# Expert 0's second layer by seven block products, with the attention pieces placed in other slots

## Chip, cores and metric

The kernel runs on one core of a Trainium2 chip. The metric is the device time of one execution in microseconds (us). A figure of a version is the median of several runs; a profile is one further execution with the hardware profiler on. The engines are called TensorE (PE in the profile, PEld for its weight loads), VectorE (DVE), ScalarE (ACT), GpSimd (POOL) and SyncE (SP). GpSimd and SyncE here mostly issue transfers (DMAs).

## What is computed

Attention over pooled keys and values, and then four "experts" of two layers each, whose outputs are summed with normalised weights:

```python
k_p = k.reshape(B, H, Sp, pool, D).mean(axis=3)      # B, H, S, D = 8, 8, 576, 64; pool = 8
v_p = v.reshape(B, H, Sp, pool, D).mean(axis=3)
scores = scale * np.matmul(q, k_p.transpose(0, 1, 3, 2))
attn = softmax(scores)
x = np.matmul(attn, v_p)                             # as (4608, 512), one row a token
p = domain_probs / (domain_probs.sum(-1, keepdims=True) + 1e-09)
for e in range(4):                                   # w1: (4, 512, 1024), w2: (4, 1024, 512)
    h = np.maximum(x @ w1[e], 0.0)
    out += p[:, e:e + 1] * (h @ w2[e])
```

The two layers of the experts are nearly all of the arithmetic.

## The kernel before

**Chunks and steps.** The 4608 tokens are nine chunks of 512: chunks 0 to 7 take 512 tokens of one batch each, chunk 8 the 64 left over of each batch (`x_rem`). A step is a chunk and an expert, `(c, e)`, 36 in all in order (`steps`, L891). In a step TensorE computes the first layer of `(c, e)` and, between its products, the second layer of the step before. Each step has two halves, `j = 0, 1`.

**First layer by seven products.** `up_seven` (L713) computes a half of the hidden tile `H_sb` by seven block products in place of eight (a Strassen-like scheme): `product` (L638) issues 8 matmuls of 256 columns. The combinations of weight blocks are made once (`combine_w1`), those of the activations per chunk (`forms_of`, four VectorE operations, L608). A product that others need too is copied from PSUM by ScalarE (`keep`, L688, into a buffer `r`), and VectorE adds it and applies the relu (`relu_sum`, L692).

**Second layer, two ways.** `down` (L816) is the plain one: for each of four rows of 128 tokens 8 matmuls of 512 columns (L823), then `merge` (L830), which scales by the token's weight. For expert 0 `merge` starts the accumulator `acc` with a scaled copy on ScalarE (L834); for the others VectorE multiplies and adds (L837); after expert 3 SyncE writes the rows out (L845). `up_down` (L744) is the other: first layer of this step and second layer of the step before, both by seven products, in an order written out by hand. Its second-layer products are calls of `half` (4 matmuls of 256 columns, L761). It needs four sums of hidden blocks (`sums_of`, L700; operations L707 to L710 on VectorE, the second of them in place in `H_sb`), made at the end of the step in which the hidden tile was finished, and combined second-layer weights `w2_t` (`combine_w2`, L624). `splits` (L697) says for which steps this holds: experts 1 and 2 (`SPLIT`, L49) in chunks 1 to 8, so `up_down` runs in the steps of experts 2 and 3, and `up_seven` with `down` in those of experts 0 and 1.

**Points and slots.** Work that is not part of this runs at points. `point` (L896) issues what is placed under the running number `at`; `slot` (L902) first takes one piece from a queue `forms_due` and then does the same. Either way of doing a step passes 16 points, every second one a slot. `attention(c)` (L536) returns the pieces for batch `b = c + 1` under a number `n`, which is placed at point `2n + 1` of the chunk: `n` 0 to 7 falls into the step of expert 0, 8 to 15 into that of expert 1, and so on. The pieces are: sums over pooled keys and values on VectorE (`key_parts`, `value_parts`), transposes by DMA on SyncE (`keys` to `kpT`, `queries` to `qT`, `turn` to `xT`), `scores` (4 matmuls and an exponential on ScalarE, L276), `context` (8 matmuls, then a reciprocal and a product on VectorE, L376, L377), loads on GpSimd, and in odd chunks the left-over tokens (`rem_queries`, `rem_scores`, `rem_context`, `rem_turn`).

**What orders the work.** Each engine does its instructions in the order of the program; semaphores order the engines. `scores`, `context` and their remainder forms share one PSUM tile of two banks (`psum_a`); `g`, `d`, `s` of a half take three banks of `psum_h`; the second layer takes three of `psum_o`. The lines that set the placing:

Of the kernel before, what the change touches and what calls it, by code (L numbers as in the profile page):

```python
# [11 lines left out]
ALU = mybir.AluOpType  # L12
# [6 lines left out]
def kernel(  # L19
# [29 lines left out]
    SPLIT = (1, 2)  # L49
# [12 lines left out]
    accpool = ctx.enter_context(tc.tile_pool(name="accpool", bufs=5))  # L62
    rpool = ctx.enter_context(tc.tile_pool(name="rpool", bufs=4))
# [37 lines left out]

    def load_later(b, half):
        load_half(b, k, "kraw", half)
        load_half(b, v, "vraw", half)
# [376 lines left out]
    def warm(n):  # L481
        bank = psum_o.tile([P, NT], F32, tag="o_ps", name="o_ps")
        for _ in range(n):
            nc.tensor.matmul(bank[:], lhsT=zeros[:, 0:P], rhs=zeros[:])
# [51 lines left out]
    def attention(c):  # L536

        lo, hi = halves
        b = c + 1
        plan = {}  # L540

        def add(n, *what):
            plan.setdefault(n, []).extend(what)

        if c % 2:
            i = c // 2
            add(18, lambda: rem_queries(i))
            add(23, lambda: rem_scores(i))
            add(26, lambda: rem_context(i))
            add(27, lambda: rem_turn(i))  # L550
        if b == B:
            for part in forms_of(B):
                add(31, part)
            return plan
        if c == 1:
            add(0, lambda: queries(b), *key_parts(b)[:2])
            add(1, *key_parts(b)[2:])
            add(1, lambda: keys(b), lambda: loads_wait(b))
            add(1, lambda: (load_q(b + 1), load_q_rem(b + 1)))
        else:  # L560
            add(0, key_parts(b)[1], lambda: keys(b))
        scored, valued, mixed = 7, 9 if c > 1 else 6, 11
        for pair in range(NPAIR):
            add(scored + pair, lambda pair=pair: scores(b, pair))
        for n, part in enumerate(value_parts(b)):
            add(valued + n, part)
        if b + 1 < B:
            add(12, lambda: queries(b + 1))
            add(17, lambda: load_later(b + 1, 0))
            if b + 2 < B:  # L570
                add(19, lambda: (load_q(b + 2), load_q_rem(b + 2)))
            add(19, lambda: load_later(b + 1, 1))
            add(30, key_parts(b + 1)[0])
        for r in range(NR):
            add(mixed + r, lambda r=r: context(b, r))
            add(mixed + 1 + r, lambda r=r: turn(b, r))
        for n, part in enumerate(forms_of(b)):
            add((20, 21, 28, 29)[n], part)
        return plan
# [103 lines left out]
    def bank():  # L683
        return psum_h.tile([P, 2, TH], F32, tag="h_ps", name="g_ps")
# [11 lines left out]

    def splits(c, e):  # L697
        return c > 0 and e in SPLIT

# [13 lines left out]
    def up_seven(c, e, j, between):  # L713

        H_sb = hidden_of(c, e)
        top, low = H_sb[:, 2 * j:2 * j + 2], H_sb[:, 4 + 2 * j:6 + 2 * j]

        g, d, s = bank(), bank(), bank()
        product(c, e, j, 1, g, True)
        r1 = keep(g)  # L720
        between(0)
        product(c, e, j, 2, s, True)
        relu_sum(top[:, :, 0:TH], s, r1)
        product(c, e, j, 6, g, False)
        r2 = keep(g)
        between(1)
        product(c, e, j, 5, d, True)
        product(c, e, j, 7, g, False)
        r3 = keep(g)
        relu_sum(low[:, :, TH:NT], d, r3)  # L730
        between(2)
        product(c, e, j, 4, g, False)
        relu(low[:, :, 0:TH], g)
        between(3)
        product(c, e, j, 3, d, False)
        later = sums_of(c, e) if j and splits(c, e) else None
        if later:
            later[0]()
        relu_sum(top[:, :, TH:NT], d, r2)
        if later:  # L740
            for part in later[1:]:
                part()

    def up_down(c, e, j, dc, de):  # L744
# [5 lines left out]
        upper, lower = slice(TH + j * P, TH + (j + 1) * P), slice(j * P, (j + 1) * P)  # L750
        acc_u, acc_l = accs[(dc, 2 + j)], accs[(dc, j)]
# [29 lines left out]
        r2 = keep(g)  # L781
        slot()
# [5 lines left out]
        add(acc_l[:], prob_l, one[:])  # L788
# [21 lines left out]
        add(acc_u[:], prob_u, two[:])  # L810
# [3 lines left out]
    sums = {}  # L814

    def down(c, e, j, n):  # L816

        first = (0, 3, 7, 12, 16)
        for at in range(first[n], first[n + 1]):
# [7 lines left out]
            if fc == FCH - 1:  # L827
                merge(c, e, r, sums[r])
# [22 lines left out]
    zeros = const.tile([P, NT], BF16, name="zeros")  # L851
    pool_map = const.tile([FR, FT, SP], BF16, name="pool_map")
    ENG = mybir.EngineType
    with tc.manual_schedule(engines={ENG.PE, ENG.DVE, ENG.Activation, ENG.Pool, ENG.SP}):
        nc.vector.memset(zeros[:], 0.0)
        nc.vector.memset(pool_map[:], 1.0)
# [3 lines left out]
        for hs in halves:  # L860
            load_first(k, "k", hs)
        nc.gpsimd.affine_select(
            out=pool_map[:], in_=pool_map[:], compare_op=ALU.is_ge, fill=0.0,
# [3 lines left out]
            out=pool_map[:], in_=pool_map[:], compare_op=ALU.is_ge, fill=0.0,  # L867
# [39 lines left out]
        for s in range(len(steps) + 1):  # L907
# [24 lines left out]
            elif s == 5:  # L932
                forms_due.extend(w[3:] + nothing[:2] + combine_w2(SPLIT[0]))
                placed.setdefault(at + 5, []).extend(combine_w2(SPLIT[1], nc.gpsimd))
# [58 lines left out]
```

## Time and profile before

| | |
|---|---|
| median of 5 runs | 518.27 us (517.82 to 519.21) |
| the profiled execution | 518.79 us, of which the span from first to last instruction is 517.1 us |
| mean granted TensorE clock | 0.996 of full |
| matmuls: L644, 256 columns | 1056 + 696 + 96 recorded, mean 272 to 273 ns |
| matmuls: L823, 512 columns | 598 recorded, mean 379 ns |
| weight loads, 128 columns | 98 ns |
| `relu_sum` L692, x166 | 687 ns |
| `keep` L688, x166 | 585 ns |
| scaled copy of expert 0, L834, x36 | 690 ns |
| accumulate of 512, L767 x64 and L837 x44 | 746 ns |
| accumulate of 256, L767 x64 | 478 ns |
| sums of hidden blocks, L707 to L710, x16 each | 685 to 692 ns |
| exponential L276, x28 | 1019 ns |

A mean of a matmul is its latency; matmuls overlap, so the pitch of a stream is shorter and is read from the starts in the order of time. Some matmul records are missing from a trace, which leaves apparent gaps of one matmul's length. Busy shares are means over the whole span; where work ends up late is read from a step's own order of time.

The busy tenths in 40 slices show TensorE at 9 almost throughout, VectorE between 4 and 8 and ScalarE between 4 and 6 after the start:

```profile
PE   8899989999999999999999999999999999999996
PEld 3656544588757875788668866886688668866883
DVE  2434889878758864877577856776578546764674
ACT  3554434655475546554565546553665346534650
```

### The profile page before, as it was taken

Reading aid. Unit: us, or ns where it says so; the run is one execution under the profiler, and the core shown is the slowest. Engines: PE = TensorE matmul, PEld = TensorE weight load, DVE = VectorE, ACT = ScalarE, POOL = GpSimd, SP = SyncE. Lnnn points to the kernel's source line nnn. Section 1 sums busy time; section 2 is a strip of 40 time slices with the busy share of each in tenths; the row PEclk is TensorE's granted clock in tenths of the full one; section 3 lists DMA queues with packets and bytes.
Section 4 is the critical chain, followed back from the end, with each engine's and each line's share of the span. In section 5 each row is a group of like instructions: output and inputs, shape, how many; then the busy total and the mean of one; then the engine's idle time right before and its main releaser. Section 6 shows DMA issues by size and latency. Waiting matters only on the chain.

```text
span 517.1 us, 10085 instructions
## 1 busy us (share of the span) xinstructions
PE 501.5 (97%) x4125; PEld 363.7 (70%) x4171; DVE 341.4 (66%) x633; ACT 267.4 (52%) x467; POOL 71.0 (14%) x81
## 2 busy tenths in 40 slices
PE   8899989999999999999999999999999999999996
PEld 3656544588757875788668866886688668866883
DVE  2434889878758864877577856776578546764674
ACT  3554434655475546554565546553665346534650
POOL 8362101812003000020030001100000000000000
PEclk9899999999999999999999999999999999999999
DMA  9999998596339232961498047701210110011003
GB/s 132 206 206 205 201 161 156 89 117 63 77 80 134 26 46 78 141 62 23 108 109 89 2 117 89 74 11 56 58 24 1 41 53 1 11 42 41 1 1 81
DMA packets 82973, 41.57 MB, mean 80 GB/s; under 512 B 46560, under 2 KB 78304, under 8 KB 82928
## 3 DMA queue, kind: packets, MB, share of 16 engines
q0 software_dynamic: 41584, 22.65, 35.2%
q1 hardware_dynamic: 41344, 18.29, 18.0%
q8 instruction: 32, 0.52, 0.4%
q14 instruction: 13, 0.11, 0.1%
HBM read 45.16 MB, written 9.44 MB: 106 GB/s over the span
## 4 chain that ended last, share of the span: by engine, by line
PE 84%; DVE 10%; issue 2%; ACT 2%; DMA 1%; POOL 1%; POOLq 0%; ACTq 0%; DVEq 0%
PE g_ps L644 34%; PE o_ps L823 24%; PE u_ps L761 17%; PE h_ps L662 3%; DVE H_sb L692 2%; DVE acc L767 2%; PE two L272 2%; PE h_ps L675 2%; PE two L395 1%; DMA q_sb<-in_q_dram 1%; DVE h_s L707 1%; DVE x_tok L377 1%; DVE acc L837 1%; DVE xf L608 1%; DVE w_t L632 0%
## 5 line engine op out<-in xcount | busy, mean ns | idle before, releaser
L644 PEld LDWEIGHTS <-w_bf 128*128 128x128 bf16 x1848 | 176.0, 98 | 45.8 <-issue 6.9
L692 DVE CUSTOM_DVE_ANT_0 H_sb<-g_ps,r 128x512 bf16<-128x512 f32 x166 | 114.0, 687 | 72.5 <-ACT r L688 52.6
L823 PE MATMUL o_ps<-w_bf,H_sb 128*128 128x512 bf16 x598 | 154.0, 379 | 2.2
L644 PE MATMUL g_ps<-xf,w_bf 128*128 128x256 bf16 x1056 | 148.4, 272 | 1.2 <-ACT g_ps L773 0.7
L688 ACT COPY r<-g_ps 128x512 f32<-128x512 f32 x166 | 97.2, 585 | 101.2 <-PE g_ps L644 97.2
L767 DVE SCALAR_TENSOR_TENSOR acc<-u_ps,p_all,acc 128x512 f32<-128x512 f32 (+1 forms) x128 | 78.0, 612 | 43.1 <-ACT u_ps L787 42.3
L644 PE MATMUL g_ps<-xT,w_bf 128*128 128x256 bf16 x696 | 99.9, 273 | 0.0
L823 PEld LDWEIGHTS <-H_sb 128*128 128x128 bf16 x640 | 62.5, 98 | 45.8
L695 ACT ACTIVATE H_sb<-g_ps 128x512 bf16<-128x512 f32 x98 | 58.4, 596 | 29.7 <-PE g_ps L644 29.7
L761 PEld LDWEIGHTS <-H_sb 128*128 128x128 bf16 x512 | 49.4, 98 | 7.1 <-DVE H_sb L708 1.3
L761 PE MATMUL u_ps<-w_bf,H_sb 128*128 128x256 bf16 x384 | 52.4, 273 | 0.2
L761 PEld LDWEIGHTS <-h_s 128*128 128x128 bf16 x384 | 37.6, 98 | 4.4
L837 DVE SCALAR_TENSOR_TENSOR acc<-o_ps,p_all,acc 128x512 f32<-128x512 f32 x44 | 32.8, 746 | 11.5 <-PE o_ps L823 11.5
L761 PE MATMUL u_ps<-w_t,h_s 128*128 128x256 bf16 x256 | 38.4, 273 | 0.0
L276 ACT ACTIVATE expT<-two 72x1024 bf16<-72x1024 f32 x28 | 28.5, 1019 | 13.4 <-PE two L272 13.4
L773 ACT COPY g_ps<-g_ps 128x512 f32<-128x512 f32 x32 | 18.3, 573 | 28.0 <-PE g_ps L644 28.0
L834 ACT ACTIVATE acc<-o_ps,p_all 128x512 f32<-128x512 f32 x36 | 24.8, 690 | 7.0 <-PE o_ps L823 7.0
L787 ACT COPY u_ps<-u_ps 128x256 f32<-128x256 f32 x32 | 11.4, 357 | 24.0 <-PE u_ps L761 24.0
L96 POOL DMA_DIRECT2D raw_kv<-in_k_dram x10 | 11.5, 1149 | 84.6 <-DVE kp L223 84.6
L96 POOL DMA_DIRECT2D raw_kv<-in_v_dram x10 | 13.0, 1298 | 73.6 <-DVE vp L223 65.8
L377 DVE TENSOR_TENSOR x_tok<-two,inv 128x512 bf16<-128x512 f32 x32 | 22.1, 692 | 1.1
L395 PEld LDWEIGHTS <-expT 72*128 72x128 bf16 x256 | 11.9, 98 | 11.0 <-DVE x_tok L377 4.8
(110 smaller groups left out, 359.6 us busy)
## 6 DMA issues: line engine op xcount, KB each, us to landing
out_dram<-acc SPq DMA_DIRECT2D x32, 256.0 KB, 2.4
w_bf<-in_moe_w_dram POOLq DMA_DIRECT2D x16, 256.0 KB, 9.8
w_bf<-in_moe_w_dram POOLq DMA_DIRECT2D x4, 1024.0 KB, 16.5
q_sb<-in_q_dram POOLq DMA_DIRECT2D x7, 512.0 KB, 8.0
raw_kv<-in_k_dram POOLq DMA_DIRECT2D x10, 288.0 KB, 7.0
raw_kv<-in_v_dram POOLq DMA_DIRECT2D x10, 288.0 KB, 9.4
raw_kv<-in_k_dram POOLq DMA_DIRECT2D x2, 576.0 KB, 15.5
w_t<-in_v_dram POOLq DMA_DIRECT2D x2, 576.0 KB, 13.4
```

What stands on the lines that cost most here:

```text
L96: nc.gpsimd.dma_start(out=raws[(nm, b)], in_=src[b].rearrange("h (j r) d -> j h r d", r=POOL)[:, :, lo:lo + POOL // 2], accum_op=ALU.add i ...
L276: nc.scalar.activation(out=state[("expT", b)][:, 2 * pair:2 * pair + 2].rearrange("j h r s p -> j s (h r) p"), in_=two[0:SP].rearrange("j ...
L377: nc.vector.tensor_tensor(out=x_tok[:], in0=c_ps[:, :, :, 0:D], in1=inv[:].unsqueeze(3).to_broadcast([P, 2, NPAIR, D]), op=ALU.mult,)
L644: nc.tensor.matmul(bank[:, t, :], lhsT=w1_bf[:, e, block, kc, lo:lo + P], rhs=x[:, kc, :], start=(first and t == 0 and kc == 0), stop=(t = ...
L688: nc.scalar.copy(out=r[:], in_=ps[:])
L692: nc.vector._custom_dve(TENSOR_ADD_SAT, out=out, in0=ps[:], in1=r[:], s0=BIG, s1=0.0)
L695: nc.scalar.activation(out=out, in_=ps[:], func=ACT.Relu)
L761: nc.tensor.matmul(out, lhsT=lhs[0][:, lhs[1] + f, lhs[2]], rhs=rhs[0][:, rhs[1] + f, rhs[2]], start=(start and f == 0), stop=(f == FCH // ...
L767: nc.vector.scalar_tensor_tensor(out=acc, in0=ps, scalar=prob, in1=acc, op0=ALU.mult, op1=ALU.add,)
L823: nc.tensor.matmul(sums[r][:], lhsT=hidden[(c, e)][:, fc, r * P:(r + 1) * P], rhs=w2_bf[:, e, fc, :], start=(fc == 0), stop=(fc == FCH - 1),)
L834: nc.scalar.activation(out=accs[(c, r)][:], in_=o_ps[:], func=ACT.Copy, scale=prob)
L837: nc.vector.scalar_tensor_tensor(out=dst, in0=o_ps[:], scalar=prob, in1=dst, op0=ALU.mult, op1=ALU.add,)
```

## The change

`SPLIT` becomes `(0, 1, 2)`, and `splits` holds for expert 0 from chunk 2 on. So the steps of expert 1 in chunks 2 to 8 become `up_down`, with the second layer of expert 0 in seven products; `combine_w2(0)` runs in step 8, the step of expert 0 in chunk 2. In `up_down` an accumulator of expert 0 is started: the lower rows by a multiply on VectorE, the upper rows by a scaled copy on ScalarE that is put off (`act_due`) to the next half, after its second `keep`. In `up_seven` the last merge of the step before is put off (`held`) until behind the sums. To make room in SBUF for the third set of `w2_t`, `acc` and `r` lose one buffer each, and `zeros` and `pool_map`, used at the start only, lie in `x_rem`. The attention pieces take other numbers `n`: scores, values and contexts come earlier, except for one context that comes later; the loads of keys are apart from those of values and come after a wait on GpSimd for `kpT`.

```diff
-    SPLIT = (1, 2)
+    SPLIT = (0, 1, 2)
...
-    accpool = ctx.enter_context(tc.tile_pool(name="accpool", bufs=5))
-    rpool = ctx.enter_context(tc.tile_pool(name="rpool", bufs=4))
+    accpool = ctx.enter_context(tc.tile_pool(name="accpool", bufs=4))
+    rpool = ctx.enter_context(tc.tile_pool(name="rpool", bufs=3))
...
+        more, far = b + 1 < B, b + 2 < B
         if c == 1:
             add(0, lambda: queries(b), *key_parts(b)[:2])
             add(1, *key_parts(b)[2:])
             add(1, lambda: keys(b), lambda: loads_wait(b))
             add(1, lambda: (load_q(b + 1), load_q_rem(b + 1)))
+            for half in range(2):
+                add(2 + half, lambda half=half: load_half(b + 1, k, "kraw", half))
+            for pair in range(NPAIR):
+                add(7 + pair, lambda pair=pair: scores(b, pair))
+            for n, part in enumerate(value_parts(b)):
+                add(6 + n, part)
+            mixed = (11, 12, 13, 14)
         else:
+            for pair in range(NPAIR):
+                add(5 + pair, lambda pair=pair: scores(b, pair))
             add(0, key_parts(b)[1], lambda: keys(b))
-        scored, valued, mixed = 7, 9 if c > 1 else 6, 11
-        for pair in range(NPAIR):
-            add(scored + pair, lambda pair=pair: scores(b, pair))
-        for n, part in enumerate(value_parts(b)):
-            add(valued + n, part)
-        if b + 1 < B:
-            add(12, lambda: queries(b + 1))
-            add(17, lambda: load_later(b + 1, 0))
-            if b + 2 < B:
-                add(19, lambda: (load_q(b + 2), load_q_rem(b + 2)))
-            add(19, lambda: load_later(b + 1, 1))
-            add(30, key_parts(b + 1)[0])
-        for r in range(NR):
-            add(mixed + r, lambda r=r: context(b, r))
-            add(mixed + 1 + r, lambda r=r: turn(b, r))
+            for n, part in enumerate(value_parts(b)):
+                add(3 + n, part)
+            if more:
+                add(0, lambda: loads_wait(b))
+                for half in range(2):
+                    add(2 + 2 * half, lambda half=half: load_half(b + 1, k, "kraw", half))
+            mixed = (9, 11, 12, 19)
+        for n, r in zip(mixed, range(NR)):
+            add(n, lambda r=r: context(b, r))
+            add(n + 1, lambda r=r: turn(b, r))
+        if more:
+            add(11, lambda: queries(b + 1))
+            add(31, key_parts(b + 1)[0])
+            for half in range(2):
+                add(17 + 2 * half, lambda half=half: load_half(b + 1, v, "vraw", half))
+        if far:
+            add(19, lambda: (load_q(b + 2), load_q_rem(b + 2)))
         for n, part in enumerate(forms_of(b)):
-            add((20, 21, 28, 29)[n], part)
+            add((22, 25, 28, 29)[n], part)
...
     def splits(c, e):
-        return c > 0 and e in SPLIT
+        return e in SPLIT and (c > 1 or c == 1 and e > 0)
...
+        later = sums_of(c, e) if j and splits(c, e) else None
+        held = [] if later else None
...
         if later:
-            for part in later[1:]:
+            for part in later[1:] + held:
                 part()
...
+        if de == 0:
+            for r in (j, 2 + j):
+                accs[(dc, r)] = accpool.tile([P, DM], F32, name="acc")
...
         r2 = keep(g)
+        while act_due:
+            act_due.pop()()
         slot()
...
-        add(acc_l[:], prob_l, one[:])
+        if de == 0:
+            nc.vector.tensor_scalar_mul(out=acc_l[:], in0=one[:], scalar1=prob_l)
+        else:
+            add(acc_l[:], prob_l, one[:])
...
-        add(acc_u[:], prob_u, two[:])
+        if de == 0:
+            act_due.append(lambda: nc.scalar.activation(
+                out=acc_u[:], in_=two[:], func=ACT.Copy, scale=prob_u))
+        else:
+            add(acc_u[:], prob_u, two[:])
...
-                merge(c, e, r, sums[r])
+                if held is not None and r == NR - 1:
+                    held.append(lambda: merge(c, e, r, sums[r]))
+                else:
+                    merge(c, e, r, sums[r])
...
-    zeros = const.tile([P, NT], BF16, name="zeros")
-    pool_map = const.tile([FR, FT, SP], BF16, name="pool_map")
+    zeros = x_rem[:, 0]
+    pool_map = x_rem[0:FR, 1, 0:FT * SP].rearrange("p (r j) -> p r j", r=FT)
...
             elif s == 5:
-                forms_due.extend(w[3:] + nothing[:2] + combine_w2(SPLIT[0]))
-                placed.setdefault(at + 5, []).extend(combine_w2(SPLIT[1], nc.gpsimd))
+                forms_due.extend(w[3:] + nothing[:2] + combine_w2(1))
+                placed.setdefault(at + 5, []).extend(combine_w2(2, nc.gpsimd))
+            elif s == 8:
+                forms_due.extend(nothing[:1] + combine_w2(0))
```

## The prediction

> **What bounds the kernel now.** I read the engines' totals and the chain of waits first (the page), then the table of waits, then the order of time on TensorE and VectorE chunk by chunk.
>
> ```profile
> PE 501.5 (97%) x4125; PEld 363.7 (70%) x4171; DVE 341.4 (66%) x633; ACT 267.4 (52%) x467; POOL 71.0 (14%) x81
> ...
> PE 84%; DVE 10%; issue 2%; ACT 2%; DMA 1%; POOL 1%; POOLq 0%; ACTq 0%; DVEq 0%
> ```
>
> TensorE carries the end: 84% of the chain is matmuls, and VectorE's 10% are short hand-overs. A microsecond of matmul that goes is a microsecond of time, unless a hand-over takes its place. From chunk 2 on, TensorE itself hardly waits; of the table of waits from 133 us on, three rows matter here:
>
> ```profile
> PEld L761 <- DVE H_sb L708: 1.3, 4, 0.4
> ...
> DVE xf L608 <- DMA xT<-x_tok: 0.6, 1, 0.6
> ...
> PE g_ps L644 <- ACT g_ps L773: 0.5, 3, 0.2
> ```
>
> (total us, times, longest.) These are the places where the new step can stumble: the sums of hidden blocks, a transposed `xT` that is late, and an exponential ahead of a copy.
>
> **1. The matmuls.** Expert 0's second layer, per chunk, is 32 matmuls of 512 columns (L823); it becomes 2 x 7 x 4 = 56 of 256 columns (L761). The order of time on TensorE (start, us, operation, count) gives step lengths:
>
> ```profile
> 414.86 1.04 PE L644 MATMUL g_ps<-xT,w_bf 128*128 128x256 bf16 x8
> ...
> 427.88 1.04 PE L644 MATMUL g_ps<-xT,w_bf 128*128 128x256 bf16 x8
> ...
> 480.22 1.04 PE L644 MATMUL g_ps<-x_rem,w_bf 128*128 128x256 bf16 x8
> ...
> 492.95 0.60 PE L644 MATMUL g_ps<-x_rem,w_bf 128*128 128x256 bf16 x4
> ```
>
> Pitches come from unbroken groups in the chain of waits in order of time: five L823 take 1.08 us (216 ns each), eight L644 take 0.87 us (109 ns). So 32 x 0.216 = 6.91 becomes 56 x 0.109 = 6.12: 0.79 us saved. The fence confirms it. The groups of eight in it are a step's last product and the next one's first, so a step starts 0.44 us after they do. Chunk 7's expert 1 step (plain second layer, no attention) lasts 427.88 - 414.86 = 13.02 us; chunk 8's expert 2 step (seven products) lasts 492.95 - 480.66 = 12.29. The difference of 0.73 has 0.05 of stall in it that every first seven-product step of a chunk has today, and that only moves. Seven chunks (2 to 8): **5.5 us saved.**
>
> A rule speaks against this. The Trainium skill, "TensorE: Matmul & The Clock Gate", section "Back-to-back issue gap", gives a sustained pitch of about 131 ns for 512 columns and 81 ns for 128 in streams of weight load and matmul. An estimate from it, on a line between the two, is 98 ns for 256 columns: 32 x 131 = 4.2 us would become 56 x 98 = 5.5, a loss of 1.3 per chunk and 9 in all. The trace has 216 and 109, which is that section's formula for the isolated gap (N/2.4 + 2.5 ns), so the measured row decides. It also shows the weight load at 98 ns under a pitch of 109: 24 more loads per chunk hide, with 11 ns to spare.
>
> **2. ScalarE and VectorE in the expert 1 step.** Per half (`j`), ScalarE had three `keep` (585), one `relu` (596) and two scaled copies (690), 3.7 us; now the copy of `s` (573), two `keep`, two `relu`, two quarter copies (362, 357) and one scaled copy, 4.3 us, of 6.1. It fits. VectorE had three `relu_sum` (687), 2.1 us; now two, one multiply of 512 (no row; between `relu_sum` 687 and the accumulate 746, I take 690) and two adds of 256 (478): 3.0. The four sums of `sums_of` (687 each, 2.75) now also follow step 0. That is 4.7 us of VectorE per chunk, 33 in all, on 341: 73% of a 515 us span, beside TensorE. What is late next is the order in it:
> - Step 1 to step 2 is now a seven-product step after a seven-product one. There the second sum (L708) must end before product 7 of the second layer. The rows: TensorE stands 0.10 us in chunk 8 (between steps 2 and 3) and 0.25 us in chunk 4, where a form of `xT` delays VectorE just before. No form is placed at the end of step 1: 0.10 x 7 = 0.7 (ends 0 and 1.75).
> - The last merge of expert 3 (746) would stand before the sums at the end of step 0; `held` moves it behind them. With it VectorE starts the first multiply about 0.6 us after its data, while its reader on TensorE (product 4) is 2 us off: nothing.
> - `acc_u` goes to ScalarE behind the next `keep`. Its bank is wanted only a half later, and the third `r` and fourth `acc` buffers come free 0.4 us or more ahead of need (`relu_sum` of product 3 against `keep` of product 6): nothing; without that cover, the 0.7 of one operation per half.
>
> **3. Attention pieces.** Same instructions, other slots (16 points a step, two to a slot). Scores move from slots 7-10 to 5-8: three of the four exponentials (1019) fall into step 0. The one in slot 7 now stands ahead of the copy of `s` at the start of step 1. Nearest row: the remainder's exponential, which does just that in odd chunks, 0.18 us of TensorE. Five chunks (2 to 6): 0.9 (ends 0 and 5 x 1.02 = 5.1). The scores need `kpT`: in chunk 4 its transpose is issued at 243.40 and lands 4.6 us later (4.9 at most) at 248.3; slot 5 stands at 249.6. It holds by 1.3 us. `key_parts(b+1)[0]` goes from slot 30 to 31, behind the same accumulate; `kp` ends no later. Value parts in slots 3, 4 fill gaps of 0.9 to 2.0 us that VectorE has in step 0.
>
> **4. Queues.** On POOL, `loads_wait` and the key halves now come first, then the value halves, `q`, `q_rem`. Rows say 6 to 9 us each to landing, and halves wait for one another: keys land some 22 us into a chunk of 53, wanted at its end; values at 35, wanted after 59. They hide. On SP, `queries` stands behind `turn(0)` and so some 2 us later within its step than today; the `q` load on POOL waits for that.
>
> **5. Once.** `combine_w2(0)`: 4 x 0.684 = 2.7 us of VectorE in step 8, where VectorE idles 4.0 us of such a step in chunk 4 (0.94, 0.41, 0.71, 2.00) and the value parts take 1.4: nothing; 2.7 without that cover. In chunk 1 the POOL half of `combine_w2` no longer waits for the values but for the first key half to land, so it starts near 96 us and not 92.94. While POOL computes, VectorE's same operations take longer: 2557, 1175, 1172 against 682. Pushed later, this could meet the sums at 105.7. No row; ends -0.8 and +1.5, I take 0.3. `zeros` and `pool_map` in `x_rem`: its first write is at 125.55; nothing (if the two parts were tracked as one, up to 3 us under loads that land near 6).
>
> **6. The late context.** Context 3 goes from slot 14 to 19, its turn to 20, the first two forms to 22 and 25 (still 4 slots or more before their products). In chunk 4's times `x_tok` would be ready at 276.36 + 0.90 = 277.3 (behind the accumulate that ends at 276.36), and VectorE reaches the form at 280.9: 3.6 us for the transpose. How long it takes depends on what else moves (four-transpose windows of chunk 6, and of chunk 3 beside loads):
>
> ```profile
> xT<-x_tok SPq DMA_TRANSPOSE x4, 2.6
> ...
> xT<-x_tok SPq DMA_TRANSPOSE x4, 6.3
> ...
> 168.65 0.42 DVE L608 TENSOR_TENSOR xf<-xT 128x512 bf16<-128x512 bf16 x1 [0.57 <-DMA xT<-x_tok]
> ```
>
> "DMA: Bandwidth & Descriptors", section "Issuing engines are not separate DMA queues", says that issues of all engines share the same 16 and interleave; the two rows agree. By the bare row the wait is nothing, by the contended row 2.7 us per chunk. What is in flight: `qT` issues about 7 us into step 1, lands 7 later, so `q` starts 1 us into step 2 and lands 6.7 to 8 later, 7.5 to 9; the transpose starts at 8.1. I take the near row plus a remnant: 0.5 in all, over chunks 2 to 4 (the ones with a `q` load).
>
> **Sum.** 5.5 - 0.7 - 0.9 - 0.3 - 0.5 = 3.1. The profiled execution took 518.79 (span 517.1 and 1.7 around it), so 515.7; the median of the runs is 0.5 lower, so **515.2**.
>
> **Rivals.**
> - *The fourth turn is late* (slower). The form blocks VectorE ahead of `relu_sum` and the sums, which have no slack there (back to back from 279 to 285), so lateness reaches TensorE in full. At 6.3 us to landing: 3 x 2.7 = 8.1, less the 0.5 counted: 522.8. It decides from 5.2 us to landing: 3 x 1.55 = 4.6, the 3.1 gained, the 0.5 counted and the 1.0 that a measurement can tell. For it: landings of 5.0 to 8.1 beside loads; against: the `q` load should be nearly done. 0.22.
> - *VectorE is the bound in steps 0 and 1* (no change). Step 0 would hold 8.9 + 1.4 + 2.75 = 13.0 of 14.4 us, step 1 2 x 3.0 + 3 x 0.9 + 2.75 = 11.5 of 13.4; the densest stretch today is 10.1 of 12.5. A lag of 0.3 at each of two boundaries in five chunks costs 3: 518.2. For it: 90% is above anything shown; against: the gaps lie before the sums. 0.13.
> - The forecast, 513 to 517: 0.65.
>
> A measurement of this kernel tells about 0.2% (1 us) from no change. Range 513.0 (all small costs nil: 512.8) to 519.6, into the first rival. Faster 0.65, same 0.13, slower 0.22.
>
> **What would show it.** 896 + 7 x 56 = 1288 matmuls of L761; step 1 of chunk 7 at 12.3 to 12.4 for 13.02. Right if L708 waits stay near 0.1 per chunk and L773 near 0.2 in chunks 2 to 6. Wrong if L608 waits for `xT` by over 1 us in chunks 2 to 4, if the scores wait for `kpT`, or if L708 waits of 0.5 appear at the start of step 1.

## The result, and the profile after

The changed kernel takes **515.33 us** (median of 27 runs, 513.89 to 520.84); the kernel before, run beside it, takes 518.73 (median of 48). The ratio is 0.9941 (0.9931 to 0.9950): 0.6% faster, 3.4 us by the medians. The forecast was 515.2. The profiled execution took 515.58 with a span of 513.8, 3.3 less than the 517.1 of before. The mean granted clock was 0.999 against 0.996; the difference lies in the stretch from 13 to 26 us, where before had 0.87 and the changed kernel 1.00. In the stretches read behind it (26 to 54, 54 to 89, 89 to 132, 133 to 510 us) both had 1.00.

The page, engines' totals, the chain's shares, and two groups (engine totals in us and share of the span; groups as busy time, mean ns | idle time before):

```profile
PE 496.4 (97%) x4312; PEld 378.8 (74%) x4339; DVE 371.1 (72%) x693; ACT 274.0 (53%) x495; POOL 72.3 (14%) x85
...
PE 77%; DMA 9%; DVE 8%; POOL 2%; issue 2%; ACT 1%; DVEq 0%; POOLq 0%; ACTq 0%
...
L807 DVE TENSOR_SCALAR acc<-u_ps,p_all 128x512 f32<-128x512 f32 x14 | 10.5, 751 | 14.1 <-ACT u_ps L805 14.1
L717 DVE TENSOR_TENSOR h_s<-H_sb 128x1024 bf16<-128x1024 bf16 x23 | 16.8, 732 | 5.3 <-ACT H_sb L703 5.3
```

TensorE's busy time fell by 5.1 us, close to the 5.5 of matmul time, and the span by only 3.3. VectorE is busy 29.7 us more. Of the chain's 9% of DMA, 8 are first loads, through which the chain now follows the start-up, and 1 is a transpose at 383 us that comes up below. The last row carries a hint: its mean is 732 ns, where 22 of the 23 take 681 to 693; one took 1766.

The waits from 133 us on (total us, times, longest), the rows that answer to those shown of before:

```profile
PEld L777 <- DVE H_sb L718: 2.9, 11, 0.6
...
PEld L777 <- DVE h_s L719: 1.0, 5, 0.2
...
PE g_ps L652 <- ACT g_ps L789: 0.5, 3, 0.2
DVE xf L616 <- DMA xT<-x_tok: 0.4, 1, 0.4
PE u_ps L777 <- DVE H_sb L718: 0.3, 1, 0.3
```

(L718 was L708, L777 was L761, L652 was L644, L789 was L773, L616 was L608.) The waits of the weight loads for the sums went from 4 to 11; TensorE itself pays for little of them, as the order of time shows. The wait behind an exponential is what it was, three times, although five more were foretold. One turn was late, by 0.4, and no scores waited for `kpT`.

The step lengths below are worked out from the order of time on TensorE (start of a step's first product to the next step's). A `product` is 4 matmuls of 256 columns, not 8 as said above: two blocks of output times two of input (L641 to L644 before). A group of eight in the order of time is two products.

| us | before | after |
|---|---|---|
| chunk 1, experts 1 / 2 / 3 | 16.54 / 13.07 / 13.06 | 16.51 / 14.65 / 13.20 |
| chunk 2, steps 0 / 1 / 2 / 3 | 13.46 / 15.41 / 12.30 / 12.47 | 14.35 / 13.53 / 12.59 / 12.48 |
| chunk 7, steps 0 / 1 / 2 / 3 | 13.03 / 13.02 / 12.78 / 13.06 | 13.03 / 12.29 / 12.82 / 13.06 |
| start of chunk 2, of chunk 8's last step | 131.91, 492.95 | 132.88, 489.81 |

Chunk 7 has no attention in its first three steps and shows the bare gain. The order of time on TensorE there (start, us):

```profile
413.11 1.04 PE L652 MATMUL g_ps<-xT,w_bf 128*128 128x256 bf16 x8
413.98 0.60 PE L777 MATMUL u_ps<-w_bf,H_sb 128*128 128x256 bf16 x4
414.49 1.03 PE L652 MATMUL g_ps<-xf,w_bf 128*128 128x256 bf16 x8
...
425.84 0.60 PE L652 MATMUL g_ps<-xT,w_bf 128*128 128x256 bf16 x4
```

The step starts in the middle of the first group, at 413.55, and the next at 425.84: 12.29 us, by seven products at the pitch that was read before. In an attention chunk step 1 gained 1.9, and step 0 lost 0.9 and step 2 0.3, because attention moved from the one to the others; chunks 2 and 4 gained 0.7 each, as much as chunks 7 and 8. Chunks 3 and 5 gained 0.56: their step 3 took 13.20 for 13.06. VectorE and TensorE there, in chunk 3:

```profile
232.46 0.42 DVE L616 TENSOR_TENSOR xf<-xT,xf 128x512 bf16<-128x512 bf16 x1
...
234.03 0.68 DVE L700 CUSTOM_DVE_ANT_0 H_sb<-g_ps,r 128x512 bf16<-128x512 f32 x1
```

```profile
234.18 0.60 PE L777 MATMUL u_ps<-w_bf,H_sb 128*128 128x256 bf16 x4
234.76 1.03 PE L652 MATMUL g_ps<-xf,w_bf 128*128 128x256 bf16 x8
```

The form that moved to slot 25 now stands ahead of the left-over tokens' context and of the `relu_sum` behind it, which ends at 234.71; TensorE, done at 234.62, goes on at 234.76. `place_only` below has the same 13.20 (in chunk 5), `split_only` has 13.06: it belongs to the places.

From chunk 2 to chunk 8's last step the changed kernel gains 4.1 us. It came into chunk 2 behind by 1.0. That is the whole account: 4.1 - 1.0 = 3.1.

### The profile page after: what moved, and what is told of

Read it like the earlier page. It is cut to its first block, busy times and chain, and to the rows that moved or that the text cites. A ratio compares the mean times of both kernels' runs of the same rounds, so it can differ in the third digit from the quotient of the medians.

```text
span 513.8 us, 10536 instructions
## 1 busy us (share of the span) xinstructions
PE 496.4 (97%) x4312; PEld 378.8 (74%) x4339; DVE 371.1 (72%) x693; ACT 274.0 (53%) x495; POOL 72.3 (14%) x85
## 4 chain that ended last, share of the span: by engine, by line
PE 77%; DMA 9%; DVE 8%; POOL 2%; issue 2%; ACT 1%; DVEq 0%; POOLq 0%; ACTq 0%
PE g_ps L652 34%; PE u_ps L777 25%; PE o_ps L850 13%; DMA w_bf<-in_moe_w_dram 4%; DMA q_sb<-in_q_dram 4%; DVE acc L783 2%; PE two L268 2%; DVE H_sb L700 1%; PE h_ps L670 1%; PE two L391 1%; DVE h_s L717 1%; POOL w_bf L148 1%; DVE x_tok L373 1%; DMA xT<-x_tok 1%; DVE xf L616 1%
## 5 line engine op out<-in xcount | busy, mean ns | idle before, releaser
L652 PEld LDWEIGHTS <-w_bf 128*128 128x128 bf16 x1848 | 176.8, 98 | 40.7 <-issue 8.0
L652 PE MATMUL g_ps<-xf,w_bf 128*128 128x256 bf16 x1056 | 148.4, 272 | 2.9 <-DVE H_sb L700 1.8
L700 DVE CUSTOM_DVE_ANT_0 H_sb<-g_ps,r 128x512 bf16<-128x512 f32 x152 | 104.3, 687 | 32.6 <-ACT r L696 29.8
L783 DVE SCALAR_TENSOR_TENSOR acc<-u_ps,p_all,acc 128x256 f32<-128x256 f32 (+1 forms) x156 | 91.4, 588 | 41.9 <-ACT u_ps L805 40.9
L652 PE MATMUL g_ps<-xT,w_bf 128*128 128x256 bf16 x696 | 101.8, 273 | 0.0
L850 PE MATMUL o_ps<-w_bf,H_sb 128*128 128x512 bf16 x393 | 99.8, 379 | 1.2
L777 PEld LDWEIGHTS <-H_sb 128*128 128x128 bf16 x736 | 70.0, 98 | 11.9 <-DVE H_sb L718 2.9
L777 PE MATMUL u_ps<-w_bf,H_sb 128*128 128x256 bf16 x552 | 75.5, 273 | 0.4 <-DVE H_sb L718 0.3
L777 PEld LDWEIGHTS <-h_s 128*128 128x128 bf16 x552 | 54.0, 98 | 6.2
L777 PE MATMUL u_ps<-w_t,h_s 128*128 128x256 bf16 x368 | 55.2, 273 | 0.0
L789 ACT COPY g_ps<-g_ps 128x512 f32<-128x512 f32 x46 | 26.3, 572 | 48.2 <-PE g_ps L652 48.1
L777 PE MATMUL u_ps<-w_t,H_sb 128*128 128x256 bf16 x184 | 27.6, 273 | 0.0
L777 PE MATMUL u_ps<-w_bf,h_s 128*128 128x256 bf16 x184 | 27.6, 273 | 0.0
L807 DVE TENSOR_SCALAR acc<-u_ps,p_all 128x512 f32<-128x512 f32 x14 | 10.5, 751 | 14.1 <-ACT u_ps L805 14.1
L717 DVE TENSOR_TENSOR h_s<-H_sb 128x1024 bf16<-128x1024 bf16 x23 | 16.8, 732 | 5.3 <-ACT H_sb L703 5.3
```

Source lines behind the costliest of these rows:

```text
L652: nc.tensor.matmul(bank[:, t, :], lhsT=w1_bf[:, e, block, kc, lo:lo + P], rhs=x[:, kc, :], start=(first and t == 0 and kc == 0), stop=(t = ...
L700: nc.vector._custom_dve(TENSOR_ADD_SAT, out=out, in0=ps[:], in1=r[:], s0=BIG, s1=0.0)
L717: lambda: add(out=s1, in0=a21, in1=a22),
L777: nc.tensor.matmul(out, lhsT=lhs[0][:, lhs[1] + f, lhs[2]], rhs=rhs[0][:, rhs[1] + f, rhs[2]], start=(start and f == 0), stop=(f == FCH // ...
L783: nc.vector.scalar_tensor_tensor(out=acc, in0=ps, scalar=prob, in1=acc, op0=ALU.mult, op1=ALU.add,)
L789: nc.scalar.copy(out=s[:], in_=g[:])
```

## The experiments

No kernel here leaves out a part of the computation. Times are medians; ratios are against the kernel before on the same chip.

**The two halves alone.** `split_only` is the changed kernel with the old attention places; `place_only` is the old kernel with the new ones.

```diff
 # split_only: attention(c) of before, in the changed kernel
-            mixed = (9, 11, 12, 19)
+        scored, valued, mixed = 7, 9 if c > 1 else 6, 11
...
-            add((22, 25, 28, 29)[n], part)
+            add((20, 21, 28, 29)[n], part)
 # place_only: the same lines the other way round, in the kernel before
```

> Expert 0 split as in the changed kernel, attention pieces at the numbers of the kernel before (scores 7-10, values 9-10, contexts 11-14, forms 20, 21, 28, 29, loads at 17 and 19). Theory (the matmuls give 0.69 us in every chunk, the new places only keep VectorE and ScalarE out of the way): chunks 7 and 8, which have no attention, keep their 0.69 each; in chunks 2 to 6 VectorE would hold about 2 x 3.0 + 1.4 + 4 x 0.9 + 2.75 = 13.8 us in a step 1 of some 14.4 us, so stalls eat 0.3 to 0.7 of each chunk: 516 to 518, and no late POOL sums in chunk 1 (1.7 less than the changed kernel there). Rival (the places do nothing for the time, TensorE is the bound anywhere): 515.3 - 1.7 = 513.6.

> The kernel before with the changed kernel's attention places alone, expert 0 not split. Theory (places are not where the gain is): no chunk gets shorter by more than 0.1 us, chunk 1 longer by about 1.7 (POOL's sums of weights run beside VectorE's sums of hidden blocks): 518.5 to 520.5. Rival (a good part of the 3.4 us comes from the places): 516 to 517.5.

`split_only` took 526.41, ratio 1.0163 (1.0139 to 1.0188): both expectations missed it by 8 to 13 us. `place_only` took 520.26, ratio 1.0034 (1.0020 to 1.0049), as its theory had it. Neither part gains by itself. Steps 0 to 2 of chunk 2 together: before 41.17, `place_only` 41.16, `split_only` 42.70, changed kernel 40.47. Without attention (chunks 7 and 8) `split_only` has its 12.29 too. So the new layer costs 1.5 per attention chunk at the old places, and the new places are worth 2.2 once it is there and nothing while it isn't. (Of `place_only`'s loss, 1.5 stands before chunk 2, which starts at 133.40, and 0.8 behind it, most of that in step 3 of chunk 3, where a form waits 1.0 for a late fourth turn.)

Where it goes in `split_only`: the waits from 133 us on, then the order of time in chunk 2's step 1, on TensorE and on VectorE.

```profile
PEld L395 <- DVE x_tok L377: 6.7, 5, 1.3
PE two L395 <- DVE x_tok L377: 5.3, 5, 1.1
PEld L769 <- DVE H_sb L710: 4.5, 11, 0.6
...
PE two L272 <- ACT expT L276: 2.9, 5, 0.6
```

```profile
152.67 0.41 PE L272 MATMUL two<-qT,kpT 64*72 64x256 bf16 x4 [0.57 <-ACT expT L276]
...
161.15 0.43 PE L395 MATMUL two<-vp,expT 72*128 72x65 bf16 x8 [1.06 <-DVE x_tok L377]
```

```profile
158.50 0.75 DVE L799 TENSOR_SCALAR acc<-u_ps,p_all 128x512 f32<-128x512 f32 x1 [0.77 <-ACT u_ps L797]
159.17 0.69 DVE L692 CUSTOM_DVE_ANT_0 H_sb<-g_ps,r 128x512 bf16<-128x512 f32 x1
159.78 0.47 DVE L775 SCALAR_TENSOR_TENSOR acc<-u_ps,p_all,acc 128x256 f32<-128x256 f32 x1
160.17 0.19 DVE L376 RECIPROCAL inv<-two 128x8 f32<-128x8 f32 x1
160.40 0.69 DVE L377 TENSOR_TENSOR x_tok<-two,inv 128x512 bf16<-128x512 f32 x1
```

In each of five chunks TensorE stands 1.1 for a context's bank, which `x_tok` has not yet read, and 0.6 for the scores' bank. VectorE isn't full: its busy time in that step is 12.8 of 16.5 us. It is held up in order: `x_tok` stands behind the new multiply, which stands still 0.77 for its own data, then behind `relu_sum` and an accumulate. In the changed kernel three contexts come ahead of that multiply and the fourth goes to step 2. This is the second rival's mechanism (VectorE late in step 1) in a sharper form: the places, not the load, decide.

**The merge that is held back.** Chunk 7's step 1 has no attention in it; `no_held` puts the last merge back ahead of the sums.

```diff
-        held = [] if later else None
+        held = None
...
-            for part in later[1:] + held:
+            for part in later[1:]:
```

> The changed kernel without the merge of the last rows held back behind the sums. Theory (the sums at the end of step 0 have no slack): the merge's 0.66 us lies ahead of them, L718 ends about 0.4 us after product 7 wants it in chunks 2 to 8: L718 waits of 0.3 to 0.5 at the start of each step 1, 517.5 to 518.5. Rival (VectorE has the slack, the hold is for show): 515.3.

519.02, ratio 1.0013 (1.0003 to 1.0024): all of the gain is gone. Step 1 of chunks 2 to 6 is 13.91 for 13.53, of chunks 7 and 8 13.12 for 12.30: 5 x 0.38 + 2 x 0.82 = 3.5 us. The loss is somewhat larger than expected (517.5 to 518.5), and the wait is not the expected one. The order of time in chunk 7, on VectorE and on TensorE:

```profile
415.03 0.75 DVE L867 SCALAR_TENSOR_TENSOR acc<-o_ps,p_all,acc 128x512 f32<-128x512 f32 x1 [0.41 <-PE o_ps L850]
415.69 0.68 DVE L717 TENSOR_TENSOR h_s<-H_sb 128x1024 bf16<-128x1024 bf16 x1
416.29 0.69 DVE L700 CUSTOM_DVE_ANT_0 H_sb<-g_ps,r 128x512 bf16<-128x512 f32 x1
```

```profile
417.03 1.03 PE L652 MATMUL g_ps<-xf,w_bf 128*128 128x256 bf16 x8 [0.73 <-DVE H_sb L700]
```

The merge waits 0.41 for the plain layer's last matmul and takes 0.75; the first sum and then `relu_sum` (L700) stand behind it, and TensorE's next product wants the bank that `relu_sum` reads. So the wait is for a bank (seven times, 2.9 us in all, 0.73 the longest), and comes one operation earlier than the wait for L718, which is what it was.

**The late fourth turn.** The first rival. `q_beside_turn` lets the `q` load on POOL wait for the fourth `x_tok`; `q_in_flight` starts it behind a hidden block some two slots earlier, so that it is in flight when the transpose is issued (the second value half goes one slot up).

```diff
 # q_beside_turn, if c > 1
+                add(19, lambda: nc.gpsimd.tensor_copy(
+                    out=mark[:], in_=state[("x", b, 3)][0:1, 0, 0, 0:1]))
 # q_in_flight, if c > 1; then load_q at 18
+                add(18, lambda: nc.gpsimd.tensor_copy(
+                    out=mark[:], in_=hidden[(c, 2)][0:1, 4, TH:TH + 1]))
```

> The changed kernel, but POOL waits for the last x_tok of chunks 2 to 4 before it issues the q load, so that the load of 512 KB and the last transpose to xT start together. Theory (what the transpose takes depends on what is in flight): its landing goes from 2.6-2.8 to 5-8 us, the form waits 1.4 to 4 us in three chunks and TensorE loses nearly all of it: 519 to 526. Rival (a transpose issued at the same time as a load hardly shares with it, or VectorE has slack behind the form): 515.3 to 516.5.

> The changed kernel, but in chunks 2 to 4 the q load (behind both value halves) waits on POOL for the relu sum in the first half of step 2, so that it is issued about 2 us ahead of the last transpose to xT and is in full flight beside it. Theory (the transpose shares the 16 DMA engines; lateness of the form reaches TensorE in full): landing 5 to 7 us, the form waits 1 to 3 us in three chunks, steps (2, 2), (3, 2), (4, 2) longer by that: 518 to 524. Rival (lateness is taken up by VectorE's slack, or one load in flight does not slow one transpose much): landing under 4 us, 515.0 to 516.5.

`q_beside_turn` missed its aim: 516.63, ratio 0.9948 (0.9935 to 0.9962). The transpose was issued 0.6 us ahead of the load, whose issue alone takes 0.92 us on POOL, and landed in 2.4 to 2.5 us; none of these forms waited. `q_in_flight` made the collision, and its theory held: 518.51, ratio 1.0000 (0.9983 to 1.0016), the transposes of chunks 2 to 4 landing in 4.6, 5.3 and 4.8 us. Its waits from 133 us on, and the order of time in chunk 3 on VectorE and TensorE:

```profile
DVE xf L619 <- DMA xT<-x_tok: 4.1, 3, 1.8
```

```profile
228.48 0.43 DVE L619 TENSOR_TENSOR xf<-xT 128x512 bf16<-128x512 bf16 x1 [1.79 <-DMA xT<-x_tok]
```

```profile
229.95 1.03 PE L655 MATMUL g_ps<-xf,w_bf 128*128 128x256 bf16 x8 [1.00 <-DVE H_sb L703]
231.28 1.05 PE L780 MATMUL u_ps<-w_bf,H_sb 128*128 128x256 bf16 x8 [0.30 <-DVE H_sb L721]
```

The form's 1.79 comes out as 1.00 and 0.30 on TensorE at once. The three steps are 1.23, 1.29 and 1.28 longer than the changed kernel's: 3.8 of 4.1 us of lateness reach the end. The rival's price was right. It isn't paid in the changed kernel, where the `q` loads start at 160.29, 218.01 and 267.35, 3.9 to 8.7 us ahead of the transposes (168.96, 221.91, 276.07), and not 2.4 ahead as in `q_in_flight`. They haven't all landed by then (170.88, 223.66, 277.04), but with only their last 1.0 to 1.9 us left the transposes land in 2.6 to 2.8 us. So a load beside the transpose does not by itself make it late.

**Chunk 1.** The 1.0 us that is lost before chunk 2. The order of time in the changed kernel, on POOL, VectorE and TensorE:

```profile
95.48 1.41 POOL L96 DMA_DIRECT2D raw_kv<-in_k_dram  x1 [9.84 <-DMA raw_kv<-in_k_dram]
96.36 2.68 POOL L640 TENSOR_TENSOR w_t<-w_bf 128x1024 bf16<-128x1024 bf16 x1
...
104.07 2.56 POOL L643 TENSOR_TENSOR w_t<-w_bf,w_t 128x1024 bf16<-128x1024 bf16 x1
```

```profile
103.48 1.18 DVE L643 TENSOR_TENSOR w_t<-w_bf,w_t 128x1024 bf16<-128x1024 bf16 x1
...
105.42 1.77 DVE L717 TENSOR_TENSOR h_s<-H_sb 128x1024 bf16<-128x1024 bf16 x1
107.11 0.68 DVE L700 CUSTOM_DVE_ANT_0 H_sb<-g_ps,r 128x512 bf16<-128x512 f32 x1
```

```profile
107.84 1.03 PE L652 MATMUL g_ps<-xf,w_bf 128*128 128x256 bf16 x8 [1.77 <-DVE H_sb L700]
```

POOL's four sums now wait for the first key half to land and run from 96.36 to 106.6; before they ended at 102.3. The first of `sums_of` meets the last of them, takes 1.77 instead of 0.68, and TensorE stands 1.77 for the `relu_sum` behind it. This meeting hangs on when the key half lands. `q_beside_turn`, `q_in_flight` and `no_loads_wait` (below) are the changed kernel up to chunk 2; in their executions POOL issues the second half at 93.3 to 93.9 and not at 95.48, step (1, 2) takes 13.56 or 13.57, and chunk 2 starts at 132.15 to 132.75. Against 131.91 before, the loss is 0.2 to 1.0 us from one execution to another. Three kernels move those sums or what they wait for:

```diff
 # keys_after, c == 1: key halves issued behind POOL's sums
-                add(2 + half, lambda half=half: load_half(b + 1, k, "kraw", half))
+                add(11 + half, lambda half=half: load_half(b + 1, k, "kraw", half))
 # sums_gated: POOL's sums one step later, behind the last of sums_of
-                placed.setdefault(at + 5, []).extend(combine_w2(2, nc.gpsimd))
+            elif s == 6:
+                placed.setdefault(at, [])[0:0] = [
+                    lambda: nc.gpsimd.tensor_copy(out=mark[:], in_=h_s[0:1, 2, 0, 0:1])
+                ] + combine_w2(2, nc.gpsimd)
...
+                add((17 if c > 1 else 12) + 2 * half, lambda half=half: load_half(b + 1, v, "vraw", half))
 # sums_gated2: the same, but the value halves at 12 and 17
+                add((17 + 2 * half) if c > 1 else (12, 17)[half], lambda half=half: load_half(b + 1, v, "vraw", half))
```

> The changed kernel, but the key loads of chunk 1 are issued at 11 and 12 in place of 2 and 3, behind POOL's sums of weights. Theory (the 1.7 us that chunk 1 lost are POOL's sums, held up in POOL's queue by the second key half, which waits for the first to land): POOL starts them near 85 us, is done by 95, VectorE's L717 takes 0.7 and not 1.77 us, step (1, 2) goes from 14.65 back to about 13.1: 513.5 to 514.0. Rival (whenever POOL computes, VectorE's slower operations cost TensorE the same somewhere else): 515.0 to 515.6.

> The changed kernel, but in chunk 1 POOL first issues the value halves (at 12 and 14) and then waits for the last of VectorE's sums of hidden blocks of step (1, 1) before it makes its own sums of weights, so that these run in step (1, 2) beside VectorE's work on PSUM. Theory (POOL's sums slow only VectorE's sums and differences in bf16 between SBUF tiles, which take 1.8 to 2.6 us in place of 0.7; the relu sums and the accumulates stay at 0.69 and 0.75): steps (1, 1) and (1, 2) fall from 31.2 together to 29.2 to 29.6, 513.5 to 514.0. Rival (POOL's 9 to 10 us cost TensorE about 1.7 wherever they lie): 515.0 to 515.6.

> As sums_gated, but the second value half is issued behind POOL's sums, so that they start when the sums of step (1, 1) end, near 107, and end near 116. Theory (POOL's sums cost only where VectorE has bf16 work between SBUF tiles; a free stretch of 8.7 us lies between the sums of step (1, 1) and the form): step (1, 3) falls from 14.76 to 13.2, chunk 2 starts near 130.0 and not at 132.9: 512.3 to 513.3. Rival (it moves to another step once more): 514.5 to 515.5.

| us | (1, 1) | (1, 2) | (1, 3) | start of chunk 2 | median, ratio (interval) |
|---|---|---|---|---|---|
| changed kernel | 16.51 | 14.65 | 13.20 | 132.88 | 515.33, 0.9941 (0.9931 to 0.9950) |
| `keys_after` | 18.30 | 12.96 | 13.19 | 132.92 | 515.15, 0.9938 (0.9926 to 0.9951) |
| `sums_gated` | 15.40 | 12.96 | 14.76 | 131.44 | 515.14, 0.9940 (0.9917 to 0.9964) |
| `sums_gated2` | 15.41 | 12.96 | 13.20 | 131.03 | 512.78, 0.9878 (0.9856 to 0.9900) |

`keys_after` pulls POOL's sums forward (the last starts at 91.41), the stall in step (1, 2) goes, and step (1, 1), where VectorE makes forms and its own sums at the same time, gets longer by 1.8. `sums_gated` clears both, but its first value half held POOL until 108.84, so that the sums ended only at 118.97 and met the next step's: the loss moved a third time, and the median can't be told from the changed kernel's. Both medians lie where their rivals said. `sums_gated2` lets the second half wait instead. Its POOL, in order of time:

```profile
108.50 2.12 POOL L640 TENSOR_TENSOR w_t<-w_bf 128x1024 bf16<-128x1024 bf16 x1
...
114.87 2.12 POOL L643 TENSOR_TENSOR w_t<-w_bf,w_t 128x1024 bf16<-128x1024 bf16 x1
```

Each takes 2.12 and not up to 2.68; only the last meets something, a form of `xT` that takes 0.73 for 0.41. All three steps are short, chunk 2 starts 1.85 us earlier, and the interval lies below those of both others. The median fell into the expected range. Chunk 2 starts at 131.03 and not near 130.0, since step (1, 1) began 0.95 later in this execution than in the changed kernel's (89.46 for 88.51). The ratios put it 3.3 us ahead of the changed kernel, the profiles 2.3: 1.85 here and 0.47 in chunk 6, whose late turn it lacks. The rest is not explained.

`scratch_before` asks whether `zeros` and `pool_map` inside `x_rem` explain that step (1, 1) began 0.7 us earlier after the change:

```diff
-    zeros = const.tile([P, NT], BF16, name="zeros")
+    zeros = x_rem[:, 0]
```

> The kernel before with zeros and pool_map laid into x_rem, nothing else. Theory (the 0.7 us by which step (1, 1) started earlier after the change is a matter of the single execution's loads): 518.2 to 518.8. Rival (it belongs to the change): 517.4 to 517.9, with step (1, 1) starting at 88.5 and not at 89.2.

519.05, ratio 1.0003 (0.9994 to 1.0011). Step (1, 1) starts at 88.33 there, as the rival said, but chunk 2 at 131.86 (before: 89.24 and 131.91): the early start is eaten within chunk 1, and the scratch costs and gains nothing. It need not be the scratch that starts it early: of these profiles only that of before had the clock of 0.87 between 13 and 26 us.

**Two small waits.** On top of `sums_gated2`, `form_behind` puts the first form of the fourth turn behind the sums (slot 23 for 22). `no_loads_wait`, from the changed kernel, drops the wait on POOL at slot 0 from chunk 2 on.

```diff
-            add((22, 25, 28, 29)[n], part)
+            add((23, 25, 28, 29)[n], part)
 # no_loads_wait, c > 1
-                add(0, lambda: loads_wait(b))
```

> As sums_gated2, and the first form of xT goes from 22 to 23, behind the sums. Theory (the form's 0.41 us ahead of the sums is what makes the L718 wait 0.25 and not 0.10, and what waits for a late transpose in chunk 6): 0.15 us in each of six chunks and 0.2 to 0.5 in chunk 6: 1.1 to 1.4 below sums_gated2. Rival (the second sum waits for something else): no difference.

> The changed kernel without POOL's wait for kpT ahead of the key loads in chunks 2 to 5. Theory (the key load beside the transpose is why kpT took 4.6 us before and takes 2.7 now, and slot 5 has 1.3 us to spare even at 4.6): kpT lands after 4.4 to 4.9 us, no wait of the scores, 515.0 to 515.8. Rival (the wait is what keeps the early scores on time): waits of TensorE for kpT at the first score of 0.5 us or more per chunk, 517 or more.

`form_behind`: 512.01, ratio 0.9871 (0.9853 to 0.9890), an interval that overlaps that of `sums_gated2`, 0.9856 to 0.9900. The gap behind the first products shrank from 0.24 to 0.09, but 0.14 came back before a later product, and step 3 stayed at 12.47. The form's 0.33 on VectorE is late by whichever reader stands behind it. Expected were 1.1 to 1.4 us; the medians differ by 0.8, which the intervals can't tell from the rival's no difference. The rival's reason failed: the form was what made the gap, and its cost only moved. `no_loads_wait`: 514.52, ratio 0.9919 (0.9899 to 0.9939), an interval that overlaps the changed kernel's; `kpT` landed in 4.7 to 5.2 beside loads (chunks 2 to 5) and still no scores waited. Its median is a little below the expected 515.0 to 515.8. The wait makes the landing quick and nobody needs that.

## Why the prediction was right, and where it wasn't

The bound and the mechanism of the gain were right. That the total was met within 0.2 us is partly luck: a term of 0.9 that came to nothing stands against 0.7 too little for chunk 1 and 0.3 that no term had.

- **Matmuls, -5.5: right.** 1288 matmuls of L777 as foretold; chunk 7's step 1 went from 13.02 to 12.29. The measured pitch of before decided rightly against the rule that spoke for a loss of 9 us.
- **The wait for the second sum, +0.7: right.** In chunk 2, boundary of steps 1 and 2:

```profile
161.64 1.04 PE L652 MATMUL g_ps<-xf,w_bf 128*128 128x256 bf16 x8
162.60 1.05 PE L777 MATMUL u_ps<-w_bf,H_sb 128*128 128x256 bf16 x8
```

  Eight matmuls take 0.87, so 0.09 is the gap; 0.10 was taken. In chunks 7 and 8 the net is -0.69 and -0.70 a chunk: 0.73 less 0.03 to 0.04 in the step behind (chunk 7's step 2 went from 12.78 to 12.82).
- **The exponential ahead of the `s` copy, +0.9: wrong, it is 0.** The row came from the remainder's exponential, which stands directly ahead of the product whose bank is copied. In slot 7 another product lies between:

```profile
146.45 0.41 PE L268 MATMUL two<-qT,kpT 64*72 64x256 bf16 x4
146.79 1.05 PE L652 MATMUL g_ps<-xT,w_bf 128*128 128x256 bf16 x8
147.67 0.60 PE L777 MATMUL u_ps<-w_bf,H_sb 128*128 128x256 bf16 x4
148.18 1.03 PE L652 MATMUL g_ps<-xf,w_bf 128*128 128x256 bf16 x8
```

  The group of eight after the scores is the last product of step 0 and the first of step 1. The extra 0.44 us, and the half of the second layer behind it, cover the exponential: no line bears a wait, and the gap ahead of the next products is 0.07, the same as in chunk 7 (413.98 to 414.49), which has no exponential there. The nearest row was near in kind and not in position.
- **POOL's sums in chunk 1, +0.3: mechanism right, size wrong in this execution.** It measured 1.6 in step (1, 2), with 0.1 more from the form in step (1, 3), and 1.0 at the start of chunk 2, since the kernel before had started step (1, 1) 0.7 later. Other executions lost 0.2 to 0.8 in all. The step named the meeting at 105.7; it happened at 105.42. The upper end given (1.5) was near; the choice in the middle had no row under it.
- **The late fourth turn, +0.5: total right by luck, place wrong.** Chunks 2 to 4, named for their `q` loads, landed in 2.6 to 2.8 us and waited for nothing. The 0.47 us fell in chunk 6, which has no load left at all: its transpose took 3.9 us and its step 3 12.94 for 12.47. In the executions of the other kernels with these places and the split that step took 12.47 to 12.72. The last section has what goes with it.
- **The terms at nothing.** `held`: right, and worth all of the gain (`no_held`). `kpT`: expected at 4.6 with 1.3 us to spare, landed in 2.7 (the transpose of chunk 4 that was read had taken 4.93). `x_rem` scratch: nothing (`scratch_before`). The multiply took 751 ns and not 690, without effect on the sum.
- **What the sum lacked.** It treated the moved attention as a cost of the split (terms 3 and 6). `split_only` shows the reverse: without the new places the split loses 8 us. The second rival, priced at no change, is this loss; it stays away because of the places. With them VectorE was busy 12.2 of 14.3 us in step 0 and 11.1 of 13.6 in step 1 of chunk 2, near the rival's own figures, and no wait of TensorE for it shows there. And no term had the form in slot 25, 0.14 in each of chunks 3 and 5.

In the profile's account: chunks 2 to 8 gained 4.1, where the steps for them (5.5 - 0.7 - 0.9 - 0.5) gave 3.4: 0.9 more from the exponential, 0.3 less from the form in slot 25, and 0.1 of small differences. Chunk 1 lost 1.0 for 0.3.

## What to carry to other kernels

Here TensorE was the bound and VectorE stood at 70%, and still a saving on TensorE arrived only when every hand-over kept its place in line. In such a kernel check, operation by operation, who stands behind a newly waiting instruction, and move the pieces together with the split, since neither part alone may gain. When a cost is borrowed from a row elsewhere, compare what stands between that row's operation and its reader as well as the duration. When GpSimd computes, look at which VectorE operations meet it; move its work to where none does, then look at the next step, since the loss likes to move.

## What the hardware showed that was not expected

**GpSimd and VectorE take turns on two-input SBUF operations.** In the changed kernel's chunk 1 four VectorE operations on bf16 blocks overlap POOL's sums, and each ends 0.55 us after the end of a POOL operation: the first of `sums_of` ends at 105.42 + 1.77 = 107.19, POOL's last sum at 104.07 + 2.56 = 106.63. An operation that takes 0.68 alone lasts 1.17 to 1.77, and POOL's 2.12 becomes 2.45 to 2.68. In `keys_after` the forms, 0.41 alone, last up to 2.85, and each that meets a POOL operation ends 0.28 to 0.29 after it. `relu_sum` and `x_tok`, which read PSUM, stay at 0.68 and 0.69 in the same stretch. That fits the Trainium skill, "SBUF — State Buffer", section "SBUF: two separate sides": the two engines share one pair of ports that is locked for a whole instruction, also by a VectorE operation with two SBUF inputs when the GpSimd operation reads SBUF. The trace agrees: whenever it began, each of these operations ends 0.13 short of its own length after POOL's end (0.55 for 0.68, 0.28 for 0.41), as if it ran only then. That is what a lock gives; two operations at half speed would not tie their ends so.

**A transpose's landing depends on its company, and one small packet is company enough.** The same four-block transpose of `x_tok` landed in 2.4 to 2.8 us in chunks 2 to 4 of the changed kernel and of `q_beside_turn`, in 4.6 to 5.3 with a 512 KB load issued 2.4 us before it (`q_in_flight`), and in 3.9 in chunk 6 of the changed kernel, which has no load left. The DMA view (packets, MB, share of the 16 engines' time) while that one was in flight, and in `place_only`, where no such packet ran, while the first of chunk 6 was:

```profile
q8 instruction: 1, 0.02, 2.3%
...
xT<-x_tok SPq DMA_TRANSPOSE x1, 3.9
```

```profile
q1 hardware_dynamic: 544, 0.13, 27.1%
...
xT<-x_tok SPq DMA_TRANSPOSE x1, 2.5
```

In chunk 6 one packet of 16 KB (0.02 MB) of the queue named `instruction` runs from 384.09 to 385.61, and packets of the transpose that start at 384.95 take up to 1.52 us, where the longest of `place_only` takes 0.05. In all executions kept here, 23 transposes of `x_tok` have no other transfer of the program beside them. The 4 without such a packet landed in 2.4 to 2.5 us; in the other 19 it ended 1.7 to 2.4 us after the issue, and they landed 1.3 to 1.6 after its end, in 3.2 to 3.9. So the late turn of chunk 6 is no mere scatter: the packet is there in every execution with the split and these places, and the later it ends, the later the transpose lands. No kernel was tried that moves it, so the link is read from the traces alone.
